# Windowed attention and a two-layer FFN on one NeuronCore: q's and k's parts made once for a pair, chunk 1's scores in split form, seven groups' weight sums late

## The chip, the cores and the metric

The kernel runs on one core of a Trainium2 chip. The metric is device time in microseconds of one execution. Verdicts compare medians of executions on the same chip.

## The reference

Attention with a causal window of 128 positions and a linear position bias over 8 batches, 8 heads, 576 positions and head size 64; its output, 4608 rows of 512, goes through a feed-forward block (512 to 2048 and back) with a piecewise quadratic nonlinearity. All in float32.

```python
scores = scale * np.matmul(q, k.transpose(0, 1, 3, 2))
bias = slopes[:, None, None] * (-np.abs(rel).astype(np.float32))[None, :, :]
mask = (rel >= 0) & (rel < window)
scores = np.where(mask, scores + bias[None], -1000000000.0)
...
return np.matmul(attn, v).astype(np.float32)
...
h = x @ w_in
g = np.where(pos, h, np.where(neg, 0.0, (h + beta) ** 2 / (4.0 * beta)))
return (g @ w_out).astype(np.float32)
```

## The kernel before

**Tiling.** The 4608 tokens are cut into nine chunks of 512. A chunk has 8 heads, taken as four *pairs* p of two heads m (p = 0 to 35, m = 0 to 71); a pair's q and k lie transposed, 128 rows by tokens, each head on 64 rows. For a head the scores of two blocks of 128 queries at a time go to one PSUM bank (`scores`), then come bias and row minimum on DVE, the exponential on ACT, transposes on TensorE (`weights_t`), triangular masks on GpSimd and the product with v (`values`).

**Split form.** A float32 operand can be written as a high part, rounded to the type float32r, and a low part, the rest. A product of split operands is a few float32r matmuls instead of one float32 matmul. The FFN has always three (high by high, high by low, low by high). Scores are made in two ways: pairs below `LIGHT` = 8 (chunks 0 and 1) take the plain float32 matmul of line 669 over all 128 rows, with the other head's rows of q set to zero by `qscale`; later pairs take the float32r matmuls of lines 671 and 672. For these the operands of head j are laid out on 128 rows: `ql` has q's high part on j's own 64 rows and its low part on the other 64, `kk` has k's high part twice, `kl` k's low part twice.

**q and k before.** `load_qk` loads a late pair's q once and each head's k twice, onto the upper and the lower 64 rows: four loads of 64 rows (line 552). `prepare_k` makes `kk` on ACT (612) and `kl` on DVE (613), once for each head on 128 rows of 640 elements; `prepare_q` makes q's high part on ACT (593) and its low part on DVE (596), once for each head on 64 rows of 512. For pairs 4 to 7 it scales q twice (585 on ACT or 586 on DVE).

**FFN.** A *sweep* over 8 groups g of the inner dimension makes each chunk's first layer. Chunk 0's sweep does it as four plain block products of a group (`plain`), later sweeps by a scheme of seven products (`PRODUCTS`) that needs sums of weight blocks, S1 to S4. Line 846 issues a product's six matmuls, lines 878 to 880 the second layer's. Sweep c runs beside the attention of chunk c+1. Weights come as float64, are loaded raw (425) and converted (450 to 463) during chunk 0's sweep. `build` rounds a block, subtracts to make the low part (511) and stores both to a scratch tensor in DRAM (514); later chunks `fetch` them (520) into a ring of ten tiles. The sums of groups below NG - `LATE` = 2 are made (499) in chunk 0's sweep; those of the other six groups in chunk 1's, for which the converted block is stored (`spill`, 480) and loaded again (`unspill`, 486).

**Order.** Nothing is issued where it stands in the code. `Plan` collects operations with their engines, estimated costs and dependences, gives each a latest start worked back from TensorE's order, and lays them out in one order for each engine; an operation with several engines in its `alts` takes one of them. All DMAs are issued by SP, in one queue in order: an issue that waits holds those behind it. DMAs are planned as 0.4 us of issue, 2.8 us of latency and bytes at 370 GB/s. `buf` names a tile and how many buffers of it there are: one for `qr`, `kk0`, `kk1`, `ql`, `kl`.

Of the kernel before, what the change touches and what calls it, by code (L numbers as in the profile page):

```python
# [14 lines left out]
ALU = mybir.AluOpType  # L15
# [281 lines left out]
def windowed_attention_then_ffn(  # L297
# [27 lines left out]
    FIRST = 1  # L325
    LATE = 6
    LO = D + 2
# [201 lines left out]
    def load_qk(p):  # L529
        c, g = divmod(p, NPAIR)  # L530
        nb = SIZES[c]
        n, t0 = nb * P, STARTS[c] * P
        st = pair.setdefault(p, {})
        rows = slice(g * P, (g + 1) * P)
        if c == 0:
            qk = buf("xp", ("B22", "T1", "T3", "T2")[p], 1, [P, 2, n], F32, f"qk_{p}")
            st["qr"], st["kr"] = (qk, 0, lambda: qk.t[:, 0]), (qk, 1, lambda: qk.t[:, 1])
            plan.op(dma(P * n * 4, lambda: DMA.dma_start(qk.t[:, 0], q[rows, :n])), (), [(qk, 0)])
            plan.op(dma(P * n * 4, lambda: DMA.dma_start(qk.t[:, 1], k[rows, :n])), (), [(qk, 1)])
            return  # L540
        qr = buf("ap", "qr", 1, [P, 4 * P], F32, f"qr_{p}")
        st["qr"] = (qr, None, lambda: qr.t[:, :n])
        plan.op(dma(P * n * 4, lambda: DMA.dma_start(qr.t[:, :n], q[rows, t0:t0 + n])), (), [qr])
        if p < LIGHT:
            kr = buf("ap", f"kr{p % 2}", 1, [P, 5 * P], F32, f"kr_{p}")
            st["kr"] = (kr, None, lambda: kr.t)
            plan.op(dma(P * (n + P) * 4, lambda: DMA.dma_start(kr.t[:, :n + P], k[rows, t0 - P:t0 + n])), (), [kr])
            return
# [23 lines left out]
    def prepare_q(p):  # L572
        c, g = divmod(p, NPAIR)
        n = SIZES[c] * P
        b, key, qr = pair[p]["qr"]
        if c == 0:
            ql = buf("xp", ("T4", "B21")[p % 2], 1, [P, 2, n], F32, f"ql_{p}")
        elif p < LIGHT:
            ql = buf("ap", "kl" if p % 2 else "ql", 1, [P, 2, 4 * P], F32, f"ql_{p}")
        else:  # L580
            ql = buf("ap", "ql", 1, [P, 2, 4 * P], F32R, f"ql_{p}")
        pair[p]["ql"] = ql
        for j in range(2):
            if p < LIGHT:
                alts = act_fn(n, lambda j=j: S.activation(ql.t[:, j, :n], qr(), AF.Copy, scale=qscale[:, g, j:j + 1]))
                alts.update(dve_fast(n, lambda j=j: V.tensor_scalar(ql.t[:, j, :n], qr(), qscale[:, g, j:j + 1], None,
                                                                    ALU.mult)))
                plan.op(alts, [(b, key)], [(ql, j)])
                continue
            scale = 2.0 ** (2 * g + j + 1) / 8.0  # L590

            def hi(j=j, scale=scale):
                S.mul(ql.t[lo_rows[j], j, :n], qr()[lo_rows[j]], scale)

            def lo(j=j, scale=scale):
                V.scalar_tensor_tensor(ql.t[hi_rows[j], j, :n], qr()[lo_rows[j]], scale,
                                       ql.t[lo_rows[j], j, :n].bitcast(F32), ALU.mult, ALU.subtract)

            plan.op(act(n, hi, 0.11), [(b, key)], [(ql, (j, 0))])
            plan.op(dve(n, lo, True), [(b, key), (ql, (j, 0))], [(ql, (j, 1))])  # L600

    def prepare_k(p):
        c = p // NPAIR
        if p < LIGHT:
            return
        n = (SIZES[c] + 1) * P
        pair[p]["kk"] = []
        kl = pair[p]["kl"] = buf("ap", "kl", 1, [P, 2, 5 * P], F32R, f"kl_{p}")
        for j, kr in enumerate(pair[p]["kr"]):
            kk = buf("ap", f"kk{j}", 1, [P, 5 * P], F32R, f"kk{j}_{p}")  # L610
            pair[p]["kk"].append(kk)
            plan.op(act(n, lambda kk=kk, kr=kr: S.copy(kk.t[:, :n], kr.t[:, :n])), [kr], [kk])
            plan.op(dve(n, lambda j=j, kk=kk, kr=kr: V.tensor_tensor(
                kl.t[:, j, :n], kr.t[:, :n], kk.t[:, :n].bitcast(F32), ALU.subtract), True), [kr, kk], [(kl, j)])

# [23 lines left out]
    def scores(m, blks):  # L639
# [17 lines left out]
        def products():  # L657
            for n, i in enumerate(blks):
                o = pt()[:, n]
                qs = slice(i * P, (i + 1) * P)  # L660
                if p < LIGHT:
                    kr = st["kr"][2]()
                    if c == 0 and i == 0:
                        for w in range(2):
                            T.matmul(o[:, w * P:(w + 1) * P], ql.t[:, j, qs], kr[:, :P],
                                     start=(w == 0), stop=(w == 1), skip_group_check=True)
                    else:
                        k0 = (i - (c == 0)) * P
                        T.matmul(o, ql.t[:, j, qs], kr[:, k0:k0 + 2 * P], start=True, stop=True)  # L669
                    continue  # L670
                T.matmul(o, ql.t[:, j, qs], st["kk"][j].t[:, i * P:(i + 2) * P], start=True, stop=False)  # L671
# [224 lines left out]
    for m in range(NH):  # L896
# [201 lines left out]
```

## Time and profile before

| | |
|---|---|
| median of 3 runs | 980.88 us (980.05 to 982.05) |
| the profiled execution | 981.28 us |
| its span, first to last instruction | 979.5 us |
| granted TensorE clock | 1.00 throughout |
| DMA queue of SP | 203.08 MB, 66.7% of 16 engines' span |

Most times below are of the profiled execution, counted from the span's start. A matmul's time in the trace is from its start to its modelled end, so those of neighbours overlap; the pace is read from starts. A plain float32 matmul shows as two records. The first layer's records start at 41 us (chunk 0), 157.55 (chunk 1), 261.22 (chunk 2) and then every 104 us.

### The profile page before, as it was taken

How to read it: one execution, taken by the hardware profiler on the slowest of the kernel's cores; microseconds unless marked ns; L12 is line 12 of the kernel's file. 1: busy time of each engine (PE TensorE's matmuls, PEld its weight loads, DVE VectorE, ACT ScalarE, POOL GpSimd, SP SyncE). 2: the span in 40 equal slices, each digit the busy share in tenths (PEclk: the TensorE clock that was granted, in tenths of full speed). 3: DMA queues.
4: the chain of work that ended last, by engine and by line, in shares of the span. 5: the costliest groups of instructions: out<-in, count | busy, mean ns of one | idle time of the engine just before them, and what ended most of it. 6: DMA issues, size and time to landing. Idle time of an engine off the chain costs nothing.

```text
span 979.5 us, 19660 instructions
## 1 busy us (share of the span) xinstructions
PE 968.8 (99%) x6496; PEld 882.1 (90%) x6496; DVE 816.7 (83%) x2140; ACT 651.1 (66%) x1620; POOL 190.6 (19%) x274
## 2 busy tenths in 40 slices
PE   9999999999999999999999999999999999999998
PEld 7899999999889999899899999998999999998987
DVE  7899999999997788878987798789877888885453
ACT  7998776767876666666865576667766666653222
POOL 2311102222221113111221122111211221310000
PEclk9999999999999999999999999999999999999999
DMA  9668895777776666666676658665866676556651
GB/s 343 257 227 282 291 305 169 223 229 229 230 239 194 191 193 213 206 189 191 184 235 197 199 168 261 191 184 174 249 194 188 188 231 201 164 153 198 186 152 43
DMA packets 103669, 204.33 MB, mean 209 GB/s; under 512 B 12305, under 2 KB 12305, under 8 KB 103569
## 3 DMA queue, kind: packets, MB, share of 16 engines
q1 hardware_dynamic: 103568, 203.08, 66.7%
q8 instruction: 53, 0.87, 0.4%
q14 instruction: 48, 0.39, 0.1%
HBM read 173.67 MB, written 29.36 MB: 207 GB/s over the span
## 4 chain that ended last, share of the span: by engine, by line
PE 90%; ACT 5%; DVE 3%; DMA 1%; issue 1%; POOL 0%; ACTq 0%; POOLq 0%; DVEq 0%
PE hA L846 18%; PE hB L846 13%; PE acc L878 13%; PE acc L879 13%; PE acc L880 13%; PE x L783 6%; PE h L846 4%; PE p L712 3%; PE s L671 3%; PE s L672 3%; ACT z L685 1%; PE s L669 1%; ACT raw L450 1%; DMA out_dram<-o 1%; ACT raw L460 1%
## 5 line engine op out<-in xcount | busy, mean ns | idle before, releaser
L878 PE MATMUL acc<-wo,gh 128*128 128x512 f32 x576 | 231.5, 402 | 0.0
L879 PE MATMUL acc<-wo,gh 128*128 128x512 f32 x576 | 227.2, 394 | 0.0
L880 PE MATMUL acc<-wo,gl 128*128 128x512 f32 x576 | 225.4, 391 | 0.0
L743 POOL TENSOR_SCALAR_AFFINE_SELECT lu<-lu 128x512 fp32r<-128x512 f32 x112 | 83.4, 744 | 564.1 <-ACT lu L736 548.7
L880 PEld LDWEIGHTS acc<-wo,gl 128*128 128x128 f32 x576 | 108.2, 188 | 25.0 <-DVE gl L866 0.3
L988 ACT COPY s<-hA 128x256 f32<-128x256 f32 x192 | 70.5, 367 | 86.4 <-PE hA L846 83.0
L685 ACT ACTIVATE z<-z,nmax 128x128 f32<-128x128 f32 x288 | 112.7, 393 | 16.2 <-DVE nmax L681 15.4
L983 DVE TENSOR_TENSOR h<-hB,s 128x256 f32<-128x256 f32 x192 | 80.2, 418 | 49.3 <-PE hB L846 30.4
L878 PEld LDWEIGHTS acc<-wo,gh 128*128 128x128 f32 x576 | 109.0, 189 | 9.1
L879 PEld LDWEIGHTS acc<-wo,gh 128*128 128x128 f32 x576 | 109.4, 190 | 8.3
L860 ACT ACTIVATE m<-m 128x512 f32<-128x512 f32 x144 | 90.6, 629 | 22.8 <-DVE m L857 21.6
L846 PEld LDWEIGHTS hA<-x_T,w_S 128*128 128x128 f32 x696 | 97.5, 189 | 8.2
L846 PE MATMUL hA<-x_T,w_S 128*128 128x256 f32 x696 | 102.1, 282 | 0.0
L862 DVE SCALAR_TENSOR_TENSOR h<-h,m 128x512 f32<-128x512 f32 x128 | 90.2, 705 | 9.8 <-ACT m L860 9.5
L866 DVE TENSOR_TENSOR gl<-h,gh 128x512 fp32r<-128x512 f32 x128 | 91.2, 712 | 2.6 <-ACT gh L363 0.7
L746 POOL TENSOR_SCALAR_AFFINE_SELECT lu<-lu 128x512 fp32r<-128x512 f32 x112 | 81.5, 751 | 0.0
L678 DVE COPY_PREDICATED s<-older,s 128x256 f32<-128x256 uint32 x144 | 60.1, 422 | 24.9 <-PE s L672 17.7
L857 DVE TENSOR_SCALAR m<-h 128x512 f32<-128x512 f32 x100 | 44.7, 447 | 35.6 <-ACT h L994 33.0
L681 DVE CUSTOM_DVE_ANT_0 z<-s,rel 128x128 f32<-128x128 f32 x288 | 71.1, 284 | 1.3
L994 ACT COPY h<-hA 128x256 f32<-128x256 f32 x64 | 23.7, 370 | 71.0 <-PE hA L846 69.6
L363 ACT CAST gh<-h 128x512 fp32r<-128x512 f32 x89 | 55.3, 622 | 21.9 <-DVE h L862 21.8
L783 PE MATMUL x<-lu,vs 128*128 128x256 f32 (+3 forms) x560 | 63.0, 259 | 0.0
(124 smaller groups left out, 2063.1 us busy)
## 6 DMA issues: line engine op xcount, KB each, us to landing
w_S<-d_S SPq DMA_DIRECT2D x232, 256.0 KB, 2.8
w_A<-d_A SPq DMA_DIRECT2D x192, 256.0 KB, 3.0
kr<-in_k_dram SPq DMA_DIRECT2D x112, 160.0 KB, 3.2
vn<-in_v_dram SPq DMA_DIRECT2D x33, 320.0 KB, 4.1
out_dram<-o SPq DMA_DIRECT2D x36, 256.0 KB, 3.4
qr<-in_q_dram SPq DMA_DIRECT2D x33, 256.0 KB, 3.3
raw<-in_moe_w_in_dram SPq DMA_DIRECT2D x16, 512.0 KB, 6.4
raw<-in_moe_w_out_dram SPq DMA_DIRECT2D x16, 512.0 KB, 6.7
```

What stands on the lines that cost most here:

```text
L685: plan.op({"ACT": (0.385, 0.48, lambda i=i: S.activation(z.t[:, i], z.t[:, i], AF.Exp, bias=nmax.t[:, i:i + 1], scale=-1.0, accum_out=sm.t ...
L743: G.affine_select(out=lu[s].t[:, 0:2 * nb:2], in_=a.bitcast(F32), pattern=[[0, nb], [-1, P]], base=0, channel_multiplier=1, compare_op=ALU ...
L746: G.affine_select(out=a, in_=a.bitcast(F32), pattern=[[0, nb], [1, P]], base=0, channel_multiplier=-1, compare_op=ALU.is_ge, fill=0.0)
L783: T.matmul(px[:rows, q0 * P:q1 * P], sv, mv.rearrange("p a w -> p (a w)"), start=(w == 0), stop=(w == len(todo) - 1), skip_group_check=True)
L846: T.matmul(o.t[:, at:at + 2 * P], w.t[:, a, kb], x.t[:, b, kb], start=start and n == 0, stop=stop and n == len(todo) - 1, skip_group_check ...
L860: plan.op(act_fn(n, lambda: S.activation(m.t, m.t, AF.Square, scale=0.5)), [m], [m])
L862: plan.op(dve(n, lambda: V.scalar_tensor_tensor(f.t, h.t, 1.0, m.t, ALU.max, ALU.min), not psum), src + [m], dst)
L866: plan.op(dve(n, lambda: V.tensor_tensor(gl.t, f.t, gh.t.bitcast(F32), ALU.subtract), True), dst + [gh], [gl])
L878: T.matmul(a.t, gh.t[:, ts], w.t[:, 0], start=first, stop=False)
L879: T.matmul(a.t, gh.t[:, ts], w.t[:, 1], start=False, stop=False)
L880: T.matmul(a.t, gl.t[:, ts], w.t[:, 0], start=False, stop=last)
L983: plan.op(dve(2 * P, lambda: V.tensor_tensor(f.t[:, key * 2 * P:(key + 1) * 2 * P], b.t[:, :2 * P], s.t, ALU.add)), [b, s], [(f, key)])
```

## The change

Three things. (1) A pair's q and k are loaded once, on 128 rows, into the second half of a two-part tile. The high part goes into the first half, the low part replaces the loaded values, each by one operation over 128 rows. DMAs from SBUF to SBUF then lay the parts out: `ql0`, `ql1` get two copies each (64 rows, one part), `kk0`, `kk1` two each (64 rows, both parts in one row of 5,120 bytes). Tiles `ql0`, `ql1`, `kk0`, `kk1`, `qr`, `kr` have one buffer each. The scale of q's high part comes from a new column tile `qs`. (2) This holds from pair 4 on, not 8: chunk 1's scores take the split form too. (`LIGHT` remains 8 for v, the attention weights and the values.) Pair 8's loads stand where all later pairs' stand. (3) `LATE` is 7: group 1's sums move to chunk 1's sweep too.

```diff
-    LATE = 6
+    LATE = 7
...
+    V.tensor_tensor(qs, qscale[:, :, 0], qscale[:, :, 1], ALU.add)
...
-        st["kr"] = [buf("ap", f"kr{j}", 1, [P, 5 * P], F32, f"kr{j}_{p}") for j in range(2)]
-        for j in range(2):
-            for r in lo_rows:
-                plan.op(dma(D * (n + P) * 4, lambda j=j, r=r, kr=st["kr"][j]: DMA.dma_start(
-                    kr.t[r, :n + P], k[g * P + j * D:g * P + (j + 1) * D, t0 - P:t0 + n])), (), [(st["kr"][j], r.start)])
+        qr = st["qr"] = buf("ap", "qr", 1, [P, 2, 4 * P], F32, f"qr_{p}")
+        kr = st["kr"] = buf("ap", "kr", 1, [P, 2, 5 * P], F32, f"kr_{p}")
+        plan.op(dma(P * n * 4, lambda: DMA.dma_start(qr.t[:, 1, :n], q[rows, t0:t0 + n])), (), [(qr, 1)])
+        plan.op(dma(P * (n + P) * 4, lambda: DMA.dma_start(kr.t[:, 1, :n + P], k[rows, t0 - P:t0 + n])), (), [(kr, 1)])
...
+        alts = act_fn(n, lambda: S.activation(hi(), qr.t[:, 1], AF.Copy, scale=qs[:, g:g + 1]))
+        alts.update(dve_fast(n, lambda: V.tensor_scalar(hi(), qr.t[:, 1], qs[:, g:g + 1], None, ALU.mult)))
+        plan.op(alts, [(qr, 1)], [(qr, 0)])
+        plan.op(dve(n, lambda: V.scalar_tensor_tensor(qr.t[:, 1].bitcast(F32R), qr.t[:, 1], qs[:, g:g + 1], qr.t[:, 0],
+                                                      ALU.mult, ALU.subtract), True), [(qr, 0), (qr, 1)], [(qr, 1)])
+        for j in range(2):
+            t = buf("ap", f"ql{j}", 1, [P, 4 * P], F32R, f"ql{j}_{p}")
...
+            for part, r in enumerate((lo_rows[j], hi_rows[j])):
+                plan.op(dma(D * n * 4, lambda j=j, t=t, part=part, r=r: DMA.dma_start(
+                    t.t[r].bitcast(F32), qr.t[lo_rows[j], part])), [(qr, part)], [(t, part)])
...
-        if p < LIGHT:
+        if c == 0:
             return
...
+        plan.op(rounded(n, lambda: kr.t[:, 0].bitcast(F32R), lambda: kr.t[:, 1]), [(kr, 1)], [(kr, 0)])
+        plan.op(dve(n, lambda: V.tensor_tensor(kr.t[:, 1].bitcast(F32R), kr.t[:, 1], kr.t[:, 0], ALU.subtract), True),
+                [(kr, 0), (kr, 1)], [(kr, 1)])
+        for j in range(2):
+            kk = buf("ap", f"kk{j}", 1, [P, 2, 5 * P], F32R, f"kk{j}_{p}")
...
+            for r in lo_rows:
+                plan.op(dma(D * n * 8, lambda j=j, kk=kk, r=r: DMA.dma_start(
+                    kk.t[r].bitcast(F32), kr.t[lo_rows[j]])), [kr], [(kk, r.start)])
...
-                T.matmul(o, ql.t[:, j, qs], st["kk"][j].t[:, i * P:(i + 2) * P], start=True, stop=False)
-                T.matmul(o, ql.t[:, j, qs], st["kl"].t[:, j, i * P:(i + 2) * P], start=False, stop=True)
+                for part in range(2):
+                    T.matmul(o, ql()[:, at], st["kk"][j].t[:, part, i * P:(i + 2) * P], start=part == 0, stop=part == 1)
...
-            early = NPAIR <= p + 2 < NH // 2 and p + 2 != LIGHT
+            early = NPAIR <= p + 2 < NH // 2
```

More of the change, by code (lines that the diff above doesn't have):

```diff
@@ L390, in windowed_attention_then_ffn @@
         G.memset(qscale[D:, g, 1:2], 4.0 ** g / 2.0)
+    qs = const.tile([P, NPAIR], F32, name="qs")
     dist = const.tile([P, P], I32, name="dist")
@@ L574, in prepare_q @@
         n = SIZES[c] * P
-        b, key, qr = pair[p]["qr"]
         if c == 0:
+            b, key, qr = pair[p]["qr"]
             ql = buf("xp", ("T4", "B21")[p % 2], 1, [P, 2, n], F32, f"ql_{p}")
[L578 to L586, printed above, removed]
+            pair[p]["ql"] = [(ql, j, lambda j=j: ql.t[:, j]) for j in range(2)]
@@ L587, in prepare_q @@
+            for j in range(2):
+                alts = act_fn(n, lambda j=j: S.activation(ql.t[:, j], qr(), AF.Copy, scale=qscale[:, g, j:j + 1]))
+                alts.update(dve_fast(n, lambda j=j: V.tensor_scalar(ql.t[:, j], qr(), qscale[:, g, j:j + 1], None,
                                                                     ALU.mult)))
                 plan.op(alts, [(b, key)], [(ql, j)])
[L589 to L600, printed above, removed]
+            return
+        qr = pair[p]["qr"]
+        def hi():
+            return qr.t[:, 0].bitcast(F32R)
+        alts = act_fn(n, lambda: S.activation(hi(), qr.t[:, 1], AF.Copy, scale=qs[:, g:g + 1]))
@@ L609, in prepare_k @@
-        for j, kr in enumerate(pair[p]["kr"]):
-            kk = buf("ap", f"kk{j}", 1, [P, 5 * P], F32R, f"kk{j}_{p}")
+        for j in range(2):
+            kk = buf("ap", f"kk{j}", 1, [P, 2, 5 * P], F32R, f"kk{j}_{p}")
             pair[p]["kk"].append(kk)
-            plan.op(act(n, lambda kk=kk, kr=kr: S.copy(kk.t[:, :n], kr.t[:, :n])), [kr], [kk])
-            plan.op(dve(n, lambda j=j, kk=kk, kr=kr: V.tensor_tensor(
-                kl.t[:, j, :n], kr.t[:, :n], kk.t[:, :n].bitcast(F32), ALU.subtract), True), [kr, kk], [(kl, j)])
+            for r in lo_rows:
+                plan.op(dma(D * n * 8, lambda j=j, kk=kk, r=r: DMA.dma_start(
+                    kk.t[r].bitcast(F32), kr.t[lo_rows[j]])), [kr], [(kk, r.start)])
@@ L651, in scores @@
         nk = len(blks)
-        ql = st["ql"]
+        qb, qkey, ql = st["ql"][j]
         def pt():
@@ L659, in products @@
                 o = pt()[:, n]
-                qs = slice(i * P, (i + 1) * P)
-                if p < LIGHT:
+                at = slice(i * P, (i + 1) * P)
+                if c == 0:
                     kr = st["kr"][2]()
-                    if c == 0 and i == 0:
+                    if i == 0:
                         for w in range(2):
-                            T.matmul(o[:, w * P:(w + 1) * P], ql.t[:, j, qs], kr[:, :P],
+                            T.matmul(o[:, w * P:(w + 1) * P], ql()[:, at], kr[:, :P],
                                      start=(w == 0), stop=(w == 1), skip_group_check=True)
                     else:
-                        k0 = (i - (c == 0)) * P
-                        T.matmul(o, ql.t[:, j, qs], kr[:, k0:k0 + 2 * P], start=True, stop=True)
+                        T.matmul(o, ql()[:, at], kr[:, (i - 1) * P:(i + 1) * P], start=True, stop=True)
                     continue
-                T.matmul(o, ql.t[:, j, qs], st["kk"][j].t[:, i * P:(i + 2) * P], start=True, stop=False)
-                T.matmul(o, ql.t[:, j, qs], st["kl"].t[:, j, i * P:(i + 2) * P], start=False, stop=True)
-        if p < LIGHT:
-            plan.op(pe(nk * 0.432, products), [(ql, j), (st["kr"][0], st["kr"][1])], [ptb])
+                for part in range(2):
+                    T.matmul(o, ql()[:, at], st["kk"][j].t[:, part, i * P:(i + 2) * P], start=part == 0, stop=part == 1)
+        if c == 0:
+            plan.op(pe(nk * 0.432, products), [(qb, qkey), (st["kr"][0], st["kr"][1])], [ptb])
         else:
-            plan.op(pe(nk * 2 * MM[256], products), [(ql, (j, 0)), (ql, (j, 1)), st["kk"][j], (st["kl"], j)], [ptb])
+            plan.op(pe(nk * 2 * MM[256], products), [qb, st["kk"][j]], [ptb])
         plan.op(dve(nk * P, lambda: V.copy_predicated(pt()[:, :nk, P:], older.unsqueeze(1).broadcast_to([P, nk, P]),
```

14 lines of the change are left out of this document (3 added, 11 removed).

## The prediction

> **What bounds the kernel now.** I read the share of busy time first, then the chain that ended last, then the span cut into stretches. The first line below gives each engine's busy time, the second the chain's shares by engine. The rest are stretches: their length, then busy time (with instruction count) on PE, PEld, DVE, ACT and POOL, granted clock, busy share of the DMA engines, GB/s.
>
> ```profile
> PE 968.8 (99%) x6496; PEld 882.1 (90%) x6496; DVE 816.7 (83%) x2140; ACT 651.1 (66%) x1620; POOL 190.6 (19%) x274
> PE 90%; ACT 5%; DVE 3%; DMA 1%; issue 1%; POOL 0%; ACTq 0%; POOLq 0%; DVEq 0%
> 14.00:53.40 39.40, 36.95 (x264) 33.16 (x262) 33.35 (x137) 38.80 (x117) 13.28 (x18) 1.00 0.79 292
> 53.40:157.50 104.10, 104.07 (x696) 95.66 (x697) 100.98 (x265) 86.29 (x198) 12.74 (x14) 1.00 0.80 271
> 157.50:261.20 103.70, 103.67 (x705) 94.52 (x705) 100.47 (x268) 76.17 (x196) 27.16 (x33) 1.00 0.71 219
> 261.20:366.00 104.80, 103.97 (x706) 94.60 (x705) 90.80 (x231) 70.14 (x174) 22.12 (x33) 1.00 0.68 204
> 366.00:470.70 104.70, 103.70 (x706) 94.50 (x705) 87.20 (x226) 69.81 (x173) 21.71 (x32) 1.00 0.66 199
> 470.70:574.30 103.60, 103.48 (x706) 94.57 (x705) 87.25 (x226) 69.79 (x173) 21.71 (x32) 1.00 0.67 201
> ```
>
> Three regimes. Up to 53.4 us ACT is full (38.80 of 39.40 us), PE is not: the start belongs to ACT, with DVE close behind. From there TensorE is the bound at full clock: it idles 0.03 us in each of chunk 0's and chunk 1's sweeps, then 0.83, 1.00 and 0.12 us. DVE stands at 97% in the first two sweeps without costing PE anything. So whatever takes PE instructions away after 53.4 us is a gain of its full size; relief of ACT or DVE there is worth at most the idle 0.8 to 1.0 us; and the DMA share, 0.66 to 0.80, is the room the new copies have.
>
> **Chunk 1's scores.** The timeline (start, length, engine, line) shows one group of scores, two blocks of one head, in the old plain form and in the split form that the later chunks have already:
>
> ```profile
> 86.94 1.02 PE L669 MATMUL s<-kr,ql 128*128 128x256 f32 x4
> 87.62 1.06 PE L846 MATMUL h<-x_B,b_A 128*128 128x256 f32 x6
> 88.52 0.40 PE L878 MATMUL acc<-wo,gh 128*128 128x512 f32 x1
> ...
> 207.06 0.86 PE L846 MATMUL hA<-x_B,b_S 128*128 128x256 f32 x6
> 207.76 0.28 PE L671 MATMUL s<-kk,ql 128*128 128x256 f32 x1
> ...
> 208.23 0.64 PE L846 MATMUL hB<-x_T,w_A 128*128 128x256 f32 x4
> ```
>
> Lengths overlap, starts don't. A product of six takes 207.76 - 207.06 = 0.70 us. Plain scores and the product behind them take 88.52 - 86.94 = 1.58, so the plain group takes 0.88. The split group takes 208.23 - 207.76 = 0.47. The saving is 0.41 us a group. Where do the groups lie? The stretches for chunk 1's plain scores alone:
>
> ```profile
> 0.00:53.40 53.40, 5.35 (x20) 1.00 0.81 294
> 53.40:157.50 104.10, 11.66 (x44) 1.00 0.80 271
> ```
>
> Four records are a group: 5 groups run in the ACT-bound start, where a shorter matmul only lengthens PE's wait, and 11 under the PE bound: 11 x 0.41 = **-4.5 us**. (All 16 would give -6.6.)
>
> **q's and k's parts once for a pair.** Rows of groups: busy us, mean ns.
>
> ```profile
> L613 DVE TENSOR_TENSOR kl<-kr,kk 128x640 fp32r<-128x640 f32 x56 | 45.9, 820 | 0.0
> L612 ACT CAST kk<-kr 128x640 fp32r<-128x640 f32 x56 | 40.3, 719 | 2.5 <-PE s L671 1.1
> L596 DVE SCALAR_TENSOR_TENSOR ql<-qr,ql 64x512 fp32r<-64x512 f32 x56 | 39.1, 698 | 1.7
> L593 ACT ACTIVATE ql<-qr 64x512 fp32r<-64x512 f32 x56 | 35.2, 629 | 1.7
> L585 ACT ACTIVATE ql<-qr,qscale 128x512 f32<-128x512 f32 x3 | 2.2, 722 | 0.0
> L586 DVE TENSOR_SCALAR ql<-qr,qscale 128x512 f32<-128x512 f32 x5 | 2.4, 473 | 0.0
> ```
>
> From pair 8 on DVE spent 2 x 0.82 + 2 x 0.70 = 3.04 us a pair and ACT 2 x 0.72 + 2 x 0.63 = 2.70; afterwards half of that. For pairs 4 to 7 the two scalings of q (0.72 on ACT or 0.47 on DVE) become two high parts, equal in number, and DVE gains 0.82 + 0.70 = 1.52 us a pair.
>
> *After the start* this balances. In chunk 0's sweep pairs 5 to 7 add 4.6 us of DVE, pair 8 takes 1.5 away, group 1's sums (below) 3.4. From the next sweep on DVE loses 6.1 us a sweep. What that is worth shows where PE waited last at a chunk's turn:
>
> ```profile
> 274.25 0.36 PE L671 MATMUL s<-kk,ql 128*128 128x256 f32 x1 [0.46 <-DVE ql L596]
> ```
>
> The bracket is PE's idle time and who ended it: just the operation that the change halves. I take the 0.83 us idle in that sweep as gone: **-0.8** (bounds -0.8 and 0). Next late there is PE itself.
>
> *In the start*, DVE has 39.40 - 33.35 = 6.05 us idle and takes 2 x 1.52 = 3.0 more for pairs 4 and 5; ACT's count stays. But those operations and a copy now stand in front of chunk 1's first scores. Bounds 0 (hidden) and +3.0 (all on the chain); nearest the idle time, I take **+0.5**.
>
> **The copies.** Per pair: four of k (64 rows x 5,120 bytes, 320 KB) and four of q (128 KB), 1,792 KB or 1.84 MB. The loads shrink from 4 x 160 + 256 KB to 320 + 256 (unchanged for pairs 4 to 7). No SBUF-to-SBUF copy is in the trace, so its occupancy is bounded from rows: two stretches (with and without attention's loads), then issues (KB each, us to landing).
>
> ```profile
> 595.00:700.00 105.00, 104.87 (x715) 95.84 (x714) 88.39 (x227) 70.57 (x175) 22.60 (x34) 1.00 0.68 204
> 875.00:945.00 70.00, 70.00 (x437) 63.05 (x437) 38.81 (x74) 25.68 (x54) 0.00 (x0) 1.00 0.63 187
> w_S<-d_S SPq DMA_DIRECT2D x232, 256.0 KB, 2.8
> kr<-in_k_dram SPq DMA_DIRECT2D x112, 160.0 KB, 3.2
> ...
> w<-d_w SPq DMA_DIRECT2D x6, 512.0 KB, 4.4
> ```
>
> Low end: 0.68/204 and 0.63/187 are both 3.3 to 3.4 us of all DMA engines per MB, so the 64-row loads in the first stretch occupy no more per byte than full ones: 6.1 us a pair. High end: 256 KB more cost 1.6 us of landing, so 1.2 are fixed; two 64-row loads issued together then take 2.0 us for 0.33 MB, 6.1 us/MB: 11.2 a pair. The first is a measure of occupancy, the second of landing in a shared queue, so I take 6.1.
>
> Steady sweeps: 0.67 x 103.6 = 69 us of DMA, plus 4 x (6.1 - 1.1 saved on k), is 89: 0.86. Chunk 0's sweep: 83 us, plus pairs 6 and 7 whole (12.2), pair 8 less its old loads (5.0), less group 1's stores (1.6), is 99 in a sweep that shrinks to 99.6. Full, without overflow. What hides the longer landings is the ring of ten weight tiles: a sweep has 56 products, 1.85 us each, so a fetch is issued some 18 us ahead and lands in 2.8. Copies also add waits to SP's queue; behind them stand these fetches:
>
> ```profile
> SPq L520 <- PE hA L846: 259.3, 204, 2.9
> ACT o L885 <- DMA out_dram<-o: 9.7, 6, 2.7
> 391.34 0.59 ACT L885 COPY o<-acc 128x512 f32<-128x512 f32 x1 [2.75 <-DMA out_dram<-o]
> ```
>
> The queue already stands waiting for PE to free slots (259.3 us in 204 waits): it is ahead, and a wait for DVE or for scores in front of a copy costs nothing. Without that cover is only what follows a landing at once: ACT's output copies at a chunk's end, held 2.75 us here, in the sweep where PE idled 1.00. For that and chunk 0's full queue I take **+0.8** (bounds 0, and the two DMA rivals below).
>
> The Trainium skill speaks against these copies: by "SBUF — State Buffer", section "Door 1: The DMA port swizzle", 64 neighbouring partitions reach 8 of the 16 ports and about 218 GB/s at best, half of full width. By that (an estimate) a pair's copies take 8.4 us, chunk 0's sweep asks for 106 us of DMA against 99.6, and +0.8 becomes about +2. The rows above show no such halving for loads from DRAM; no run so far shows a copy.
>
> **Group 1's sums late.** Four sums, their parts and four stores move from chunk 0's sweep to chunk 1's; four fetches go, two spills and one 512 KB load come. Bytes balance.
>
> ```profile
> L499 DVE TENSOR_TENSOR S<-w 128x256 f32<-128x256 f32 x16 | 6.9, 430 | 0.0
> L511 DVE TENSOR_TENSOR b_S<-S,b_S 128x256 fp32r<-128x256 f32 x32 | 13.2, 418 | 0.6 <-ACT b_S L363 0.3
> SPq L480 <- DVE w L463: 18.7, 8, 4.1
> 152.53 0.32 SPq L486 DMA_DIRECT2D w<-d_w  x1
> ```
>
> 4 x 0.43 + 4 x 0.42 = 3.4 us of DVE move into a sweep that loses 6.1: **0**. The two spills may hold SP's queue 2.3 us each (18.7 over 8 waits), with group 4's raw weights behind, not yet due. The first reload was issued at 152.53 us; group 1's turn in chunk 1 comes a group (13 us) after 157.5, so it has its time. Cover gone, PE would wait for those 3.4 us.
>
> **Sum.** -4.5 - 0.8 + 0.5 + 0.8 + 0 = -4.0. The profiled execution took 981.28 us (its span of 979.5 and 1.8 around it), 0.40 above the median of the runs, so 977.3 for such an execution, **976.9** for the median of 980.88.
>
> **Rivals.**
> 1. *Everything counts.* The start tightens too, so that all 16 groups pay (-6.6), and both sweeps' idle time goes (-1.8): 972.5. For it: DVE and ACT loads fall at every turn; against: the start is ACT's, and ACT loses nothing there.
> 2. *Longer start.* Pair 4's and 5's added 3.0 us lie on the path: -4.5 - 0.8 + 3.0 + 0.8 = -1.5, 979.4. For it: DVE held the chain before ACT did, up to 14 us; against: 6 us idle.
> 3. *Chunk ends.* A fuller queue makes the output stores land later, ACT is held at every turn as at 391 us, and PE loses another 1.0 us at six more: -4.0 + 6 = 982.9. Against: ACT has shed 5 us a sweep.
> 4. *DMA becomes the bound: slower.* If copies occupy over (103.6 - 69)/4 + 1.1 = 9.8 us a pair, the steady sweeps no longer fit. At 11.2, each of seven asks for 110 us, 6 too many. Chunk 0's asks for 114 against 99.6; its cover is that of the last group's raw weights:
>
> ```profile
> L425 SPq DMA_DIRECT2D raw<-in_moe_w_in_dram x2: 333/378/422, 129.6 to 130.6; - x2
> ...
> DMA to landing us min/median/max: 5.6/6.1/7.5
> ...
> 145.74 0.72 PE L846 MATMUL h<-x_B,b_A 128*128 128x256 f32 x4
> ```
>
> They land by 138.1 and are first multiplied at 145.74: 7.6 us, conversions among them. So 7 x 6 + 7 - 4 = +45, 1026; just over the point it starts at about 983.
>
> 5. *The change doesn't do what it says:* scores wait for copies instead. A pair has 26 us for load, two parts and copies that need some 14, so I give it no chance of its own.
>
> **Chances.** Forecast 0.50, first 0.18, second 0.14, third 0.10, fourth 0.08. Faster by over 0.2% (2 us, about what a measurement of this kernel can tell from no change): most of the forecast (0.46), the first, a fifth of the second: 0.67. Same: the rest of the forecast, most of the second, half of the third: 0.19. Slower: 0.14. The forecast's own range is 974 to 979; holding the others but the far part of the fourth gives 972 to 984.
>
> **What would show it.** Right: split scores (four records in 0.47 us) from the first group of chunk 1; PE without idle after about 53 us; DMA share about 0.86 in steady sweeps and up to 1.0 in chunk 0's; DVE some 6 us less a sweep. Wrong: PE waiting for copies, for weight fetches or raw weights; ACT held longer at output copies; PE's last idle time later than 53 us.

## The result

The changed kernel takes 1028.07 us (median of 4 runs, 1018.01 to 1031.89) against 980.53: ratio (of the means) 1.0465, 95% interval 1.0402 to 1.0529. It is slower by 47 us, outside the predicted range of 972 to 984. Its profiled execution took 1028.74 us, with a span of 1027.0.

The profile after, first the busy times, the queue and the chain's shares by engine, from the page:

```profile
PE 982.8 (96%) x6496; PEld 889.1 (87%) x6496; DVE 787.9 (77%) x2111; ACT 613.0 (60%) x1546; POOL 181.1 (18%) x274
q1 hardware_dynamic: 118976, 252.64, 83.5%
PE 58%; DMA 19%; DVE 11%; ACT 4%; SPq 4%; issue 2%; POOL 0%; DVEq 0%; ACTq 0%; POOLq 0%
```

DVE and ACT lost the work that they were to lose (28.8 and 38.1 us), but of the chain that ended last DMA has 19% instead of 1%. The stretches of the changed kernel (start, then sweeps 0 to 3; columns as in the prediction) show where the time goes:

```profile
0.00:53.40 53.40, 43.03 (x283) 38.80 (x283) 40.43 (x163) 41.89 (x124) 14.24 (x36) 0.97 0.98 315
53.40:170.80 117.40, 109.42 (x734) 99.96 (x734) 104.97 (x272) 91.46 (x211) 11.88 (x15) 0.97 0.95 301
170.80:282.00 111.20, 106.75 (x705) 95.83 (x704) 101.42 (x278) 72.23 (x188) 25.79 (x33) 0.98 0.90 267
282.00:391.10 109.10, 105.63 (x706) 94.95 (x705) 83.93 (x223) 65.31 (x170) 20.39 (x33) 1.00 0.88 254
391.10:499.00 107.90, 104.41 (x706) 94.81 (x705) 82.34 (x223) 63.66 (x162) 21.52 (x33) 1.00 0.86 249
```

Sweep 0 ends at 170.8 us instead of 157.6 (+13.2), sweep 1 takes 111.2 instead of 103.7 (+7.5), sweeps 2 to 8 together 745.0 instead of 718.3 (+26.7). In the later sweeps no engine is full and the DMA share is 0.86 to 0.88: nothing there is short of capacity. Sweeps 2 to 8 in one row each, before and then after:

```profile
261.20:979.50 718.30, 712.47 (x4777) 648.60 (x4775) 572.77 (x1431) 441.94 (x1087) 135.12 (x192) 1.00 0.64 192
282.00:1027.00 745.00, 723.55 (x4777) 654.47 (x4775) 541.04 (x1401) 407.39 (x1026) 129.19 (x192) 0.99 0.80 231
```

Of the 26.7 us, 15.6 are idle time of TensorE (21.4 instead of 5.8) and 11.1 are longer busy time. A part of the latter is the clock, which was 1.00 throughout before. After, seven stretches of 3.4 us inside the span have a granted clock of 0.50, three of them in these sweeps. Two of the seven:

```profile
265.40:268.80 3.40, 3.40 (x15) 3.11 (x15) 3.00 (x10) 1.63 (x6) 2.14 (x3) 0.50 0.74 253
538.50:541.90 3.40, 3.40 (x14) 3.14 (x13) 2.59 (x9) 2.17 (x7) 0.00 (x0) 0.50 0.42 110
```

Each of the seven begins within 1.1 us of the end of a wait of TensorE of 1.5 to 4.7 us; not every such wait brings one (the one shown below, of 3.15 us, doesn't). At half clock a stretch loses at most 1.7 us, so by this estimate the clock takes at most 12 of the 47 us, and 5 of the 26.7. That the waits bring it is read from the order in time alone. The rest of the longer busy time is not explained.

The waits of the changed kernel (who, for whom: us in all, times, longest) show where TensorE's idle time comes from:

```profile
DVE kr L603 <- ACT kr L363: 45.9, 20, 4.7
ACT kr L363 <- DMA kr<-in_k_dram: 30.2, 10, 4.7
PE hA L842 <- ACT s L982: 17.5, 13, 3.2
ACT kr L363 <- DMA qr<-in_q_dram: 14.1, 6, 4.0
```

L363 is k's high part on ACT, L603 its low part on DVE. One place in the steady sweeps, around 425 us, shows the mechanism. SP's queue first (start, length, engine, line, operation, count), then ACT, then TensorE; a bracket is idle time and who ended it:

```profile
417.02 1.11 SPq L610 DMA_DIRECT2D kk<-kr  x2
...
419.91 1.72 SPq L593 DMA_DIRECT2D ql<-qr  x2
...
424.90 0.33 SPq L546 DMA_DIRECT2D kr<-in_k_dram  x1
...
427.01 0.33 SPq L545 DMA_DIRECT2D qr<-in_q_dram  x1
```

```profile
424.69 0.59 ACT L732 CAST lu<-p 128x512 fp32r<-128x512 f32 x1 [1.33 <-PE p L708]
430.00 0.72 ACT L363 CAST kr<-kr 128x640 fp32r<-128x640 f32 x1 [4.72 <-DMA kr<-in_k_dram]
430.63 0.37 ACT L982 COPY s<-hA 128x256 f32<-128x256 f32 x1
```

```profile
427.26 0.64 PE L668 MATMUL s<-kk,ql 128*128 128x256 f32 x4
431.05 0.98 PE L842 MATMUL hA<-x_B,w_S 128*128 128x256 f32 x6 [3.15 <-ACT s L982]
```

The next pair's k is loaded into the one tile `kr`, so its load (424.90) waits until the copies out of it, issued at 417.02, have been carried out. The load lands near 430. ACT's order has k's high part next and ACT stands 4.72 us before it; behind it in that order is the PSUM copy `s` (L982) of a product that ran from 425.13 to 426.01, and for that copy TensorE stands 3.15 us.

### The profile page after: what moved, and what is told of

The parts are those of the page before. It is cut to its first block, busy times and chain, and to the rows that moved or that the text cites. A ratio compares the mean times of both kernels' runs of the same rounds, so it can differ in the third digit from the quotient of the medians.

```text
span 1027.0 us, 19957 instructions
## 1 busy us (share of the span) xinstructions
PE 982.8 (96%) x6496; PEld 889.1 (87%) x6496; DVE 787.9 (77%) x2111; ACT 613.0 (60%) x1546; POOL 181.1 (18%) x274
## 3 DMA queue, kind: packets, MB, share of 16 engines
q1 hardware_dynamic: 118976, 252.64, 83.5%
## 4 chain that ended last, share of the span: by engine, by line
PE 58%; DMA 19%; DVE 11%; ACT 4%; SPq 4%; issue 2%; POOL 0%; DVEq 0%; ACTq 0%; POOLq 0%
PE hA L842 13%; PE hB L842 10%; PE acc L874 8%; PE acc L875 8%; PE acc L876 8%; DMA ql<-qr 7%; DMA qr<-in_q_dram 4%; PE s L668 4%; PE x L779 4%; DMA raw<-in_moe_w_in_dram 2%; PE p L708 2%; DMA kk<-kr 2%; SPq L593 2%; DMA w_A<-d_A 1%; DMA kr<-in_k_dram 1%
## 5 line engine op out<-in xcount | busy, mean ns | idle before, releaser
L739 POOL TENSOR_SCALAR_AFFINE_SELECT lu<-lu 128x512 fp32r<-128x512 f32 x112 | 79.0, 705 | 611.2 <-ACT lu L732 595.4
L681 ACT ACTIVATE z<-z,nmax 128x128 f32<-128x128 f32 x288 | 113.1, 394 | 41.2 <-DVE nmax L677 40.8
L982 ACT COPY s<-hA 128x256 f32<-128x256 f32 x192 | 70.6, 368 | 76.9 <-PE hA L842 75.3
L977 DVE TENSOR_TENSOR h<-hB,s 128x256 f32<-128x256 f32 x192 | 80.4, 419 | 34.7 <-PE hB L842 21.4
L862 DVE TENSOR_TENSOR gl<-h,gh 128x512 fp32r<-128x512 f32 x128 | 88.7, 696 | 2.6 <-ACT gh L363 1.1
L668 PE MATMUL s<-kk,ql 128*128 128x256 f32 x512 | 82.3, 287 | 4.6 <-DVE gh L722 1.5
L668 PEld LDWEIGHTS s<-kk,ql 128*128 128x128 f32 x512 | 72.7, 194 | 8.8 <-issue 1.9
L742 POOL TENSOR_SCALAR_AFFINE_SELECT lu<-lu 128x512 fp32r<-128x512 f32 x112 | 79.1, 730 | 0.0
L603 DVE TENSOR_TENSOR kr<-kr 128x640 fp32r<-128x640 f32 x32 | 27.6, 861 | 51.2 <-ACT kr L363 45.9
```

Source lines behind the costliest of these rows:

```text
L668: T.matmul(o, ql()[:, at], st["kk"][j].t[:, part, i * P:(i + 2) * P], start=part == 0, stop=part == 1)
L681: plan.op({"ACT": (0.385, 0.48, lambda i=i: S.activation(z.t[:, i], z.t[:, i], AF.Exp, bias=nmax.t[:, i:i + 1], scale=-1.0, accum_out=sm.t ...
L739: G.affine_select(out=lu[s].t[:, 0:2 * nb:2], in_=a.bitcast(F32), pattern=[[0, nb], [-1, P]], base=0, channel_multiplier=1, compare_op=ALU ...
L742: G.affine_select(out=a, in_=a.bitcast(F32), pattern=[[0, nb], [1, P]], base=0, channel_multiplier=-1, compare_op=ALU.is_ge, fill=0.0)
L862: plan.op(dve(n, lambda: V.tensor_tensor(gl.t, f.t, gh.t.bitcast(F32), ALU.subtract), True), dst + [gh], [gl])
L977: plan.op(dve(2 * P, lambda: V.tensor_tensor(f.t[:, key * 2 * P:(key + 1) * 2 * P], b.t[:, :2 * P], s.t, ALU.add)), [b, s], [(f, key)])
```

## Experiments

All runs in one table: time (median), ratio of the means to the kernel before on the same chip with its 95% interval, and from the profiled run the first layer-1 product, the end of sweep 0, the length of sweep 1, and sweeps 2 to 8 together (us). The profiled run lies 5 us above the median in e2 and e7 and 2.3 us below it in e5 and e8.

| | time | ratio | first | sweep 0 ends | sweep 1 | 2 to 8 |
|---|---|---|---|---|---|---|
| before | 980.53 | 1 | 41.0 | 157.6 | 103.7 | 718.3 |
| after | 1028.07 | 1.0465 [1.0402, 1.0529] | 46.5 | 170.8 | 111.2 | 745.0 |
| e1 | 990.60 | 1.0097 [1.0083, 1.0111] | 47.5 | 160.7 | 108.7 | 718.9 |
| e2 | 1002.97 | 1.0229 [1.0205, 1.0254] | 48.5 | 170.9 | 114.0 | 721.6 |
| e3 | 1010.33 | 1.0300 [1.0285, 1.0315] | 39.1 | 175.8 | 114.5 | 717.5 |
| e4 | 1030.08 | 1.0498 [1.0483, 1.0512] | 47.2 | 169.6 | 116.9 | 740.5 |
| e5 | 990.15 | 1.0085 [1.0071, 1.0099] | 48.4 | 161.6 | 106.8 | 717.7 |
| e6 | 983.82 | 1.0029 [1.0018, 1.0040] | 40.9 | 157.9 | 105.7 | 719.9 |
| e7 | 1015.76 | 1.0350 [1.0325, 1.0375] | 44.1 | 157.2 | 113.6 | 747.9 |
| e8 | 988.75 | 1.0078 [1.0063, 1.0093] | 44.5 | 160.8 | 108.5 | 715.5 |
| e10 | 983.40 | 1.0028 [1.0017, 1.0039] | 40.8 | 157.3 | 107.2 | 717.0 |
| e11 | 979.69 | 0.9986 [0.9977, 0.9994] | 44.8 | 156.4 | 106.6 | 715.2 |
| e12 | 986.16 | 1.0049 [1.0036, 1.0062] | 46.5 | 155.5 | 113.4 | 716.6 |
| e13 | 980.68 | 0.9995 [0.9986, 1.0004] | 41.3 | 157.4 | 103.8 | 718.0 |
| e14 | 978.70 | 0.9979 [0.9968, 0.9990] | 46.0 | 156.4 | 104.7 | 715.9 |
| e15 | 981.08 | 0.9997 [0.9984, 1.0009] | 46.0 | 155.5 | 105.0 | 718.8 |

### The copies, or the rest? And the order they are planned in

**e1: the kernel before with split scores from pair 4 and `LATE` 7, no copies.** The second and third part of the change alone.

```diff
-    LATE = 6
+    LATE = 7
...
-        if p < LIGHT:
+        if c == 0:
             return
```

> The kernel before with the split scores from pair 4 on and LATE 7, but q's and k's parts made and loaded in the old way: parts two and three of the change without the copies. If the copies and what hangs on them are the whole loss, this takes what the forecast gave to the scores: 974 to 978 us. If the split scores or the late sums cost something themselves (DVE, which gets 3.04 us a pair more for pairs 4 to 7), it lies at or above 985 us.

990.60 us. The copies cause some 37 of the 47 us and all of the loss in sweeps 2 to 8. But without them the rest is no gain: it loses 9 us, 3.2 by the end of sweep 0 and 5.0 in sweep 1.

**e2 and e3: the changed kernel, planned for later landings.** The same operations; only the planner's guess of when the loads and copies of q and k land is raised, by 2 us (e2), by 4 for loads and 5 for copies (e3). (With the order some operations also change between DVE and ACT, 27 in e3.)

```diff
-                n.end = pipe + 0.2
+                n.end = pipe + 0.2 + n.lag
...
-                    kk.t[r].bitcast(F32), kr.t[lo_rows[j]])), [kr], [(kk, r.start)])
+                    kk.t[r].bitcast(F32), kr.t[lo_rows[j]])), [kr], [(kk, r.start)]).lag = 2.0
```

> The changed kernel with one thing told to the planner: q's and k's loads and the copies land 2 us later than its formula says. The program has the same instructions; only their order in each queue differs. Theory A (ACT and DVE stand in order before the high part of k, because its load waits for the copies out of the same single buffer to land, and PE waits for the copies of products queued behind): with the order laid out for the true landings most of the loss goes, 985 to 1000 us. Theory B (the DMA engines carry 24% more bytes than they can deliver in time): the bytes are the same, so it stays at 1015 us or more.

> As the run before with 5 us for the copies and 4 us for the loads. Theory A: the waits of ACT for k's load, 30 us now, go to below 5 us and the time to 976 to 988 us. Theory B: 1015 us or more.

Neither time reaches what theory A gave, 1002.97 and 1010.33 us. But ACT's wait for k's load, 30.2 us in the changed kernel, is 1.7 in e2 and gone in e3, and the loss in sweeps 2 to 8 shrinks from 26.7 to 3.3 and to nothing. The loss up to the end of sweep 1 doesn't: 282.0 becomes 284.9 and 290.3. (In e3 17 us of sweep 0 are at half clock, which adds to it.) Two causes, then: one that planning cures, one early that it doesn't.

What is late early on is the raw weights. The chain of waits of the changed kernel (start, length, what) leads from them to TensorE's two longest waits in sweep 0, of 3.7 and 4.7 us, which end at 53.0 and 156.4 us:

```profile
36.85 13.62 DMA raw<-in_moe_w_in_dram
50.49 0.65 ACT raw L452
...
52.42 0.52 ACT x_B L363
...
148.25 5.79 DMA raw<-in_moe_w_in_dram
...
156.38 3.55 PE x L779 x16
```

ACT waits 17.3 us for raw weights in that sweep, 6.5 before the change and 4.1 in e15 below, at a DMA share of 0.98 in the start and 0.95 after it. Here too other work stands in order behind the late operand, in the first case `x_B`, which the first layer needs.

**e4: the loads get tiles of their own.** `qi` and `ki` are loaded, the parts go to `qr` and `kr`; the ring of weight tiles shrinks from 10 to 8 to make room.

```diff
+        ki = st["ki"] = buf("ap", "ki", 1, [P, 5 * P], F32, f"ki_{p}")
...
-            t = buf("ring", "r", 10, [P, nb, P], F32, f"vn_{p}")
+            t = buf("ring", "r", 8, [P, nb, P], F32, f"vn_{p}")
```

> The changed kernel with q and k loaded into tiles of their own, so that a pair's load need not wait for the last pair's copies to land; the ring of weight tiles shrinks from ten to eight to make room. Theory A: ACT's wait for k's load goes, but the high part now waits for the copies that read the old one; the chain is one landing shorter, so half of the loss goes, about 1000 us. Theory B: bytes are the same, 1015 us or more, and with a shorter ring PE waits for weight tiles.

Nothing gained. (The shorter ring is a second difference, but TensorE shows no wait for a weight tile.) The wait only changes its name: the high part no longer waits for the load but, as it overwrites `kr`, for the copies themselves. From its waits:

```profile
ACT kr L363 <- DMA kk<-kr: 47.3, 22, 6.3
DVE kr L605 <- ACT kr L363: 19.2, 15, 3.6
```

**e7 and e8: copies only from pair 8, planned as in the change (e7) or for later landings (e8).** Chunk 1's scores stay plain and `LATE` 6, so that the steady sweeps can be seen without the start. (The last two lines are e8's alone.)

```diff
+    FROM = 8
...
+        if p < FROM:
+            kr = buf("ap", f"kk{p % 2}", 1, [P, 5 * P], F32, f"kr_{p}")
...
-                    t.t[r].bitcast(F32), qr.t[lo_rows[j], part])), [(qr, part)], [(t, part)])
+                    t.t[r].bitcast(F32), qr.t[lo_rows[j], part])), [(qr, part)], [(t, part)]).lag = 5.0
```

> The changed kernel's copies from pair 8 on only: chunk 1 plain, LATE 6, planner as it was. Theory A: the start and chunk 0's sweep are as before (41 and 116 us), the sweeps from chunk 2 on lose what they lost in the changed kernel, some 27 us: 1003 to 1010 us. Theory B (bytes): the same, since the bytes of these sweeps are those of the changed kernel; the next run tells.

> As the run before, with the planner told that copies land 5 us later and the loads 4 us later than its formula. Theory A: the sweeps from chunk 2 on lose nothing, 978 to 983 us. Theory B: no different from the run before, above 1000 us.

The same bytes and operations take 747.9 and 715.5 us in sweeps 2 to 8. (e7 loses 9.9 us in sweep 1 as well, where the first copies run, and so lies above the 1003 to 1010 us of its theory A.) One sweep of each, e7 (sweep 3) and then e8 (sweep 3):

```profile
384.20:491.00 106.80, 104.55 (x706) 94.74 (x705) 82.08 (x219) 64.57 (x164) 20.90 (x32) 1.00 0.87 252
```

```profile
372.90:476.40 103.50, 103.50 (x706) 94.71 (x706) 83.36 (x220) 63.91 (x164) 23.06 (x32) 1.00 0.93 260
```

In e8 TensorE has no idle time, at a DMA share of 0.93, and the copies land even later. From the list of DMA issues of the whole run (count, KB, median us to landing), e7 and then e8:

```profile
kk<-kr SPq DMA_DIRECT2D x112, 320.0 KB, 4.8
```

```profile
kk<-kr SPq DMA_DIRECT2D x112, 320.0 KB, 6.1
```

So in these sweeps it is neither DMA capacity nor a late landing by itself that costs, but an order of ACT and DVE laid out for earlier landings. With an honest order the copies cost nothing there. That the 2.9 us below before are a gain of theirs is not shown: kernels that change nothing in these sweeps lie from 2.4 below (e14) to 1.6 above (e6). As a whole e8 still loses 7.6 us, more than expected, up to the end of sweep 1; why was not found.

### Why the copies land late

**e9: copies by themselves.** No part of the reference is computed: sixteen SBUF copies of 64 rows by 5,120 bytes, sixteen of 128 rows by 2,560 (the same bytes), then loads from DRAM of 64 and of 128 rows.

```diff
+    for n in range(N):
+        i, j, r = n // 4, n % 4 // 2, n % 2
+        DMA.dma_start(dst[half[r], n], src_a[half[j]])
...
+    for n in range(N):
+        DMA.dma_start(dst[:, n, :W // 2], src_b[:, :W // 2])
```

> Nothing of the computation: one queue moves 5.2 MB in each of four stages, one after another: 64-row copies between SBUF tiles as in the change (5,120 bytes a row), the same bytes as 128-row copies, as 64-row loads from DRAM (2,560 bytes a row) and as 128-row loads. Theory E (64 rows reach half of the ports, so a copy holds the DMA engines twice as long per byte; estimate by the Trainium skill's SBUF page, section on the port swizzle, 218 GB/s): the first and third stage take about 24 us, the second and fourth 13 to 15. Rival (occupancy per byte is the same, as I took it for the prediction, 3.3 us a MB): all four take 13 to 17 us.

The page's row of GB/s over 40 slices of 3.2 us:

```profile
GB/s 0 0 0 0 0 0 0 175 225 241 233 229 230 230 221 237 245 382 398 394 397 226 210 255 247 102 169 324 391 406 336 47 382 381 383 380 381 384 380 208
```

About 230 in the 64-row stage, 395 in the 128-row stage, then some 250 and 400 for the loads. The landings in the trace say the same: sixteen 64-row copies from 27.33 to 48.72 us, 1.43 apart (229 GB/s); the 128-row ones from 56.21 to 68.86, 0.84 apart (389 GB/s). From first issue to last landing the first stage takes 25.3 us, the second 17.7 and the fourth 16.3, nearer to theory E (24, and 13 to 15) than to its rival (13 to 17 for all). The third was not a stage of its own: half of its 32 loads were issued before the 128-row copies had landed. Its last sixteen land 0.67 us apart, 245 GB/s. At 229 GB/s the 1.84 MB of a pair's copies occupy the engines 8.0 us; at 398, the highest slice, it would be 4.6.

**e15: the changed kernel with copies over 128 rows.** As many copies, the same bytes, the same planning; but each copy takes one part of both heads, or half of q's columns, which gives scores of other rows. (A copy's rows are half as long, 2,560 and 1,024 bytes.)

```diff
-            for r in lo_rows:
-                plan.op(dma(D * n * 8, lambda j=j, kk=kk, r=r: DMA.dma_start(
-                    kk.t[r].bitcast(F32), kr.t[lo_rows[j]])), [kr], [(kk, r.start)])
+            for part, r in enumerate(lo_rows):
+                plan.op(dma(D * n * 8, lambda kk=kk, part=part: DMA.dma_start(
+                    kk.t[:, part].bitcast(F32), kr.t[:, part])), [kr], [(kk, r.start)])
```

> The changed kernel with every copy over 128 rows instead of 64: the same number of copies, the same bytes and the same order of work, but laid out wrongly, so that scores are of other rows than they should be. By e9 such a copy occupies the DMA engines 0.82 us per 320 KB instead of 1.43, 4.6 us a pair instead of 8.0. Theory E (half the ports) for the start and chunk 0's sweep: DMA is full there (0.96 over the sweep), the two to four pairs' copies cost 3.4 us a pair less, so the first sweep ends 5 to 10 us earlier (170.8 now), and the landing of a pair's copies comes earlier by 2 to 4 us, which gives back a part of the 27 us in the later sweeps: 1005 to 1018 us. Rival, the order alone (landings of any kind come later than planned): sweep 0 stays at 122 to 124 us and the time within 5 us of 1028.

981.08 us: the whole loss is gone, more than I expected, by the end of sweep 0 too (155.5 against 170.8). From the queue's line and the issues of e15:

```profile
q1 hardware_dynamic: 135360, 252.64, 78.4%
...
kk<-kr SPq DMA_DIRECT2D x128, 320.0 KB, 3.7
```

The same 252.64 MB take 0.784 x 979.2 = 768 us of the engines instead of 0.835 x 1027.0 = 858: 2.8 us less for each of 32 pairs. The landing of k's copies falls by 1.1 us, from 4.8 to 3.7, and that is enough for the order to hold. Its waits:

```profile
ACT kr L363 <- DMA kr<-in_k_dram: 10.2, 10, 1.9
...
DVE kr L603 <- ACT kr L363: 7.1, 11, 1.8
```

They were 30.2 and 45.9 us. The planner counts every DMA's bytes at 370 GB/s; that fits a 128-row copy and is 1.6 times too fast for a 64-row one. Half rate with that plan is `after` (and e7), full rate with it e15, half rate with a plan for late landings e8: only the first loses the steady sweeps. But e15 is no gain on before either: the forecast's 4 us are missing with full-rate copies too.

### Why the split scores gave nothing

**e5, e6 and e10: one small part alone, on the kernel before.** e5 has only the split scores from pair 4, e10 only from pair 6, e6 only `LATE` 7 (one number). e5's and e10's edits, in this order:

```diff
-        if p < LIGHT:
+        if c == 0:
             return
```

```diff
+    SPLIT = 6
...
-        if p < LIGHT:
+        if p < SPLIT:
```

> The kernel before with the split scores from pair 4 on, old loads and preparation, LATE 6: the second part alone. The run without copies lost 9 us: its first product of chunk 0 came 6.5 us later, chunk 0's sweep was 3.2 us shorter, chunk 1's 5 us longer. Theory C (the parts for pairs 4 and 5 lie on ACT and DVE while these set the start): first product again at 46 to 48 us, 983 to 986 us in all, chunk 1's sweep as before. Rival (the split scores are a gain, the sums were the loss): 974 to 978 us.

> The kernel before with LATE 7 alone. Theory D (the sums of group 1 in chunk 1's sweep cost 5 us there, through the reloads that follow each other in one free buffer and DVE, which is full): 984 to 988 us, chunk 1's sweep near 108.7 us. Rival (that loss came from the split scores' preparation): 980 to 982 us.

> The kernel before with split scores for pairs 6 and 7 only, old loads and preparation, LATE 6. Theory C (pairs 4 and 5 cost the start): first product at 41 us as before, eight groups of scores shorter by 0.41 us: 977.5 to 979.5 us. Rival (any split pair in chunk 0's sweep costs as much as it saves): 980 to 985 us.

All three lose: 9.0, 2.7 and 2.5 us. e10 went as its rival said, e5 and e6 as neither theory. The stretch of sweep 1, in e5, then e6, then e10:

```profile
161.70:268.50 106.80, 104.68 (x706) 94.69 (x705) 103.80 (x274) 79.73 (x204) 29.55 (x32) 1.00 0.71 225
```

```profile
157.90:263.60 105.70, 104.84 (x706) 94.62 (x705) 103.28 (x282) 75.72 (x196) 26.85 (x33) 1.00 0.69 218
```

```profile
157.30:264.50 107.20, 104.77 (x705) 94.80 (x705) 104.25 (x275) 81.41 (x204) 28.87 (x32) 1.00 0.69 220
```

TensorE's busy time rises by about 1 us, DVE's from 100.47 to 103.3 and more; each sweep is 2.4 to 3.0 us longer than DVE's work, much as before (103.7 and 100.47). That suggests that DVE is the second bound there, though the margin isn't fixed: sweep 1 of e11 (below) takes 106.6 us with 99.57 of DVE.

**e13 and e14: the same without DVE's added work.** e10 (e13) and e5 (e14) with the low parts of q and k of chunk 1's split pairs left out of the computation; GpSimd writes zeros in their place.

```diff
+            if p < LIGHT:
+                plan.op(pool(n * 0.00114 + 0.07, lambda j=j: G.memset(kl.t[:, j, :n].bitcast(F32), 0.0)), (), [(kl, j)])
+                continue
```

> The kernel of e10 (split scores from pair 6, the parts made as before the change), with the low parts of pairs 6 and 7 left out of the computation: GpSimd fills them with zeros, so DVE loses 2 x 3.04 = 6.1 us of work and TensorE does the same as in e10. Theory D, DVE is the second bound of the sweeps of chunks 0 and 1 (97% in each of them in every kernel that lost there), so that the split form moves 0.41 us a group off TensorE onto a full DVE: with the 6.1 us gone the 8 split groups pay their 3.3 us, sweep 1 ends at 257 to 260 us instead of 264.5, 977 to 979 us in all, below the kernel before. Rival, the loss is in TensorE's order or in ACT's parts: still 983 to 984, sweep 1 ending at 264.

> The same in the kernel of e5 (split scores from pair 4): the low parts of pairs 4 to 7 left out, 12.2 us less of DVE. Theory D: the sweeps of chunks 0 and 1 together shrink from 220.1 to 214 to 216 us (their TensorE work in e5 was 109.4 + 104.7 = 214.1); the start keeps ACT's part of its loss (first product at 45 to 48 us against 41 before, since pairs 4 and 5 still have ACT's high parts in front of chunk 0), so 981 to 985 us against 990. If the start's loss is DVE's too, the first product comes at 41 to 43 us and the time is 976 to 979. Rival, not DVE: 988 to 991.

With 6.1 and 12.2 us taken off DVE, 983.40 becomes 980.68 and 990.15 becomes 978.70. So the loss of e5 and e10 hangs on DVE's low parts; that much is shown. Whether by their amount or by their place in the order is not, since the zeros also wait for no high part. The full saving is not there even now: e13 was expected at 977 to 979 and has only lost its loss. In e14 the first two sweeps shrink to 215.1 us, as expected, but the first product comes 5.0 us later, and they end at 261.0, as before (261.2). TensorE is busy 251.5 us up to there instead of 256.4: the split form takes 4.9 us off it, and 2.6 of them return as idle time in the start, 1.7 in sweep 0. (That e14 is 2.2 us faster than before comes from sweeps 2 to 8, in which it changes nothing.) Sweep 0 of e13 and of e14:

```profile
53.40:157.40 104.00, 102.72 (x711) 94.78 (x712) 96.49 (x256) 89.65 (x203) 16.19 (x21) 1.00 0.82 275
```

```profile
53.40:156.40 103.00, 101.24 (x703) 93.49 (x704) 96.61 (x258) 95.19 (x218) 19.53 (x20) 1.00 0.85 285
```

TensorE, which had been full there before, now idles 1.3 and 1.8 us; what stops it then was not tried (ACT stands at 92% in e14's row, and in e13 the chain of that stretch has 6.7% of waiting for raw weights).

### Versions

**e11 and e12: copies from pair 12 on, planned for late landings; chunks 0 to 2 make their parts in the old way.** In e11 chunk 1's scores are plain, in e12 they are split from pair 6. `LATE` is 6.

```diff
+    SPLIT = 8
+    FROM = 12
```

> Copies from pair 12 on only, with the planner told of landings 5 and 4 us later; chunks 0 to 2 in the old way, LATE 6. The run with copies from 8 lost 3.5 us in the start and 4.8 in chunk 1's sweep and gained 2.9 in the later sweeps. Theory A: the loss goes where the copies go, the gain of about 2 us in the later sweeps stays: 977.5 to 981 us. Rival (copies delay something in each sweep that the late planning only moves): above 983 us.

> Both of the last two: split scores from pair 6 on in the old way, copies from pair 12 on, planned late. If the two gains add, 974 to 978 us, below both kernels; if the start moves with the new layout of tiles, 980 to 985 us.

e11 is faster than both kernels, by 0.14% (0.06 to 0.23%) against before: sweeps 2 to 8 gain 3.1 us, sweep 1 gives 3.0 back and sweep 0 ends 1.1 earlier. As e14 gains 2.4 us in the same sweeps without copies, the 3.1 can't be put down to the copies alone. e12 adds split scores and loses 6.5 us on e11, nearly all of it in sweep 1 (113.4 against 106.6, with 6.8 us at half clock): the gains don't add.

## Why the prediction was wrong

**What failed: the copies' term, +0.8, by its size and by its mechanism.** I asked whether the copies fit into the DMA engines. For the steady sweeps the number was near, 0.86 of busy share forecast and 0.86 to 0.88 in those shown above, but by luck: these are shares of 108 to 109 us, so 93 to 96 us of DMA instead of 89, and in e8's sweep of 103.5 us the share is 0.93. Occupancy I took at 6.1 us a pair; e9 gives 8.0. That is still under the 9.8 from which I had put the DMA bound of a steady sweep, but chunk 0's sweep, which I had called full without overflow, then asks for 83 + 16.0 + 6.9 - 1.6 = 104 us against 99.6. The cost came from the time at which transfers land, with ACT and DVE working through an order planned for earlier landings (ACT stood 4.72 us in front of one rounding). The sentence that fails is "a wait for DVE or for scores in front of a copy costs nothing". It looked at SP's queue of weight fetches only: these stayed ahead, and TensorE shows no wait for a weight fetch. It did not look at what stands behind `kr`'s next load: ACT's and DVE's order, where a rounding planned too early holds PSUM copies that TensorE needs. Undoing only the half rate (e15) takes the 47 us away.

**Why the half rate was missed.** I argued from two stretches with 3.3 to 3.4 us of DMA per MB that 64-row transfers occupy no more per byte. The 64-row loads are 2.6 MB of some 21 MB in a sweep; at 250 instead of 400 GB/s they add some 4 us to 105, 0.04 of a share in which writes and the fixed parts of transfers vary as much. The row could not tell. The Trainium skill, "SBUF — State Buffer", section "Door 1: The DMA port swizzle", puts 64 neighbouring partitions at 8 of 16 ports and about 218 GB/s at best. e9 agrees with the halving: 229 GB/s, 5% above that figure, against 389. The +2 that I worked out from it was as far off as my +0.8, since it too asked for capacity alone.

**Split scores, -4.5: not got.** The group is as short as forecast (two starts 0.47 us apart in the changed kernel: 97.08 and 97.55), but "whatever takes PE instructions away after 53.4 us is a gain of its full size" was wrong. DVE stood at 97% in the same sweeps, and the pairs' parts are DVE's; e5 and e10 lose, and lose no more when the low parts are taken off DVE (e13, e14). With copies at full rate (e15) the first two sweeps end 0.7 us earlier than before, instead of 4.5.

**Chunk turns, -0.8: not shown.** Sweep 2 takes 104.1 us in e15 and 104.7 before, but 104.1 in e14 too, which relieves DVE of nothing there, and over sweeps 2 to 8 e15 gains nothing (718.8 against 718.3).

**Start, +0.5:** the first product comes 5.5 us later, beyond the bound of 3.0, but that was the wrong place to look. In e14 and e15 it also comes 5.0 later and sweep 0 still ends 1.2 and 2.1 earlier than before. What counts is the end of sweep 0, +13.2, and that is the copies' rate: DMA is at 0.98 and 0.95 there, raw weights come late, planning cures nothing (e2, e3), full-rate copies cure all (e15). (The working also counts pair 5's DVE time twice, in the start and in sweep 0; no term of the sum hangs on it.)

**Group 1's sums late, 0:** alone they cost 2.7 us (e6), 2.0 in sweep 1, where DVE without the relief of the parts rises to 103.28 us; that this is the reason was not tried. Their price inside the change was not measured by itself.

**Rivals.** The fourth gave up to 1026, and the time is 1028, but that is luck for the most part: 42 of the 49 us that it adds were to come from steady sweeps short of DMA capacity, and they weren't, as e8 shows with the same bytes. Its few microseconds for chunk 0's sweep, with raw weights that come late, fit what is seen there. The fifth, given no chance because a pair has 26 us for some 14 us of steps, was nearest for the steady sweeps, though the scores themselves waited only 1.3 us for a copy. It counted one pair's steps and not the single buffers, by which one pair's copies hold back the next pair's load. The third is not seen: ACT's waits for output stores are 9.5 us, 9.7 before.

## What to carry to other kernels

Where a schedule is laid out ahead from estimates, a new kind of transfer needs its measured landing time in that estimate before its bandwidth is argued about: an engine that stands before a late operand holds everything behind it in its order. With single buffers follow the loop (copy out, next load, rounding, next copy) and ask which engine stands in it and what that engine does for the bottleneck. And an engine at 97% beside a bottleneck at 100% is to be taken as a second bound: moving work from one to the other lost 2.5 and 9.0 us here (e10, e5).

## Not expected of the hardware

Copies between SBUF tiles over 64 rows move 229 GB/s and over 128 rows 389, in a slice up to 398 (e9), though upper and lower halves alternated as targets in the queue: halves in sequence don't add up to the full rate. Loads from DRAM on 64 rows show the same, some 250 against 400. A median landing of k's copies 1.1 us longer (4.8 against 3.7) went with 1028 instead of 981 us, while 6.1 us cost nothing where the order allowed for it (e8's later sweeps). And seven waits of TensorE of 1.5 to 4.7 us went with 3.4 us at half clock each in the changed kernel, while a wait of 3.15 us did not.
